# The second product as three float32r products, with all work in one list of steps

## The chip, the cores and the metric

The kernel runs on one core of a Trainium2 chip. Its time is the device time in microseconds (us) of one execution of the whole program. Before the change three executions took 589.52, 584.69 and 587.59 us, a median of 587.59 us.

The core has five engines, each with its own queue of instructions. TensorE multiplies matrices; the profile shows its matmuls as PE and the loading of their stationary operand as PEld. VectorE is DVE, ScalarE is ACT, GpSimd is POOL, and SyncE (SP) starts most of the DMA transfers. An engine works through its queue in order, and an instruction whose input is not there yet holds up everything behind it on that engine.

## The reference

Two parts follow each other. The first is a gated recurrence over 768 time steps, for 4 batches and 8 heads of 48 numbers; the second is a two-layer block on all 3072 tokens:

```python
f = 1.0 / (1.0 + np.exp(-f_logit))
for t in range(S):
    state = f[:, :, t, :, None] * state + np.einsum('bhd,bhe->bhde', k[:, :, t], v[:, :, t])
    y[:, :, t] = np.einsum('bhd,bhde->bhe', q[:, :, t], state)
...
h = x @ w_in                                                # (3072, 384) @ (384, 2048)
sp = np.maximum(h, 0.0) + np.log1p(np.exp(-np.abs(h)))
g = h * erf(sp)
return (g @ w_out).astype(np.float32)                       # (3072, 2048) @ (2048, 384)
```

`x` is `y` with the heads side by side, so a token has 384 numbers. The second product of the title is `g @ w_out`. Inputs and output are float32, except the two weight matrices, which come as 64-bit floats and are rounded to float32 on the chip.

## The kernel before

**Tiles and stages.** The 3072 tokens are 24 chunks of 128 (six to a batch); two chunks make a block of 256 tokens, so there are 12 blocks. For each chunk the recurrence is done as matrix products: running sums of the logarithms of the gates (`log_sums`, `tiled_sums`), their exponentials (`decays`), `q` and `k` scaled by them (`times_q`, `times_k`) and transposed, scores (`scores`, masked by `mask`), a state carried from half chunk to half chunk (`state_products`, `add_state`, copied by `copy_state`), and the rows of `x` (`x_rows`, `copy_x`). For each block, `half_group` makes the hidden values `h` in four groups of 512 hidden channels (six matmuls with 256 moving columns for half a group). A group then passes through a chain that changes between ACT and DVE: `copy_h` out of PSUM, an exponential and two tanh terms on ACT (`first`, `a_term`), two products on DVE (`times`, line 171), a tanh on ACT (line 677), and the last product on DVE (line 680), which leaves `g` in the place of `h`.

**The second product before.** Blocks 0 and 1 are multiplied plainly (`project_tile`, line 823): 32 float32 matmuls of 384 moving columns each. Blocks 2 to 11 use Strassen's rule in Winograd's form (`project`, line 870): seven products of half size in place of eight, 56 float32 matmuls of 192 columns for a block. The rule needs sums: `sum_w` makes four of `w_out` once, `sum_h` makes four of each group of `g` (DVE, line 761), and the seven products are put together by additions on DVE (line 878) and a copy on ACT (line 886).

**Weights.** `w_in` and `w_out` arrive as 16 pieces of 64-bit words. `round_piece` turns each into float32 by one pass on ACT and six on DVE (lines 346 to 369).

**What sets the order.** Until block 2's product the order of all work is the written list `EARLY`, a string of steps such as `h0_2` (block 0, half group 2) or `r5_3` (piece 5, rounding step 3). After it a loop over blocks takes the order from rules: the matmuls of `project(it - 2)` and then those of block `it + 1` are the slots, and at certain slots the loop calls `act_step` (one step of the ACT and DVE chain), `sum_step` (one sum) or `burst` (a whole chunk's recurrence work). PSUM, the memory that matmuls write to, is handed out by pools with rotating buffers: two pairs of banks for the products (`ps_moe`), one for the scores (`sc_all`), one for the rest.

**Start.** Until the first real matmuls are ready, `keep_busy` gives TensorE products of a constant tile with itself.

Of the kernel before, what the change touches and what calls it, by code (L numbers as in the profile page):

```python
# [44 lines left out]
FP32 = mybir.dt.float32  # L45
I32 = mybir.dt.int32
# [23 lines left out]
EXP_LN = 6  # L70

# [4 lines left out]
def kernel(  # L76
# [41 lines left out]
    w_out_sb = fixed("w_out_sb", [P, n_ft, d_model])  # L118
# [61 lines left out]
    xpool = main.enter_context(tc.tile_pool(name="xpool", bufs=2))  # L180
    epool = main.enter_context(tc.tile_pool(name="epool", bufs=2))
# [3 lines left out]
    singles = ExitStack()  # L185
    ps_at = [singles.enter_context(tc.tile_pool(name="ps_at", bufs=2, space=PSUM))]

    def bank(name):
        if len(ps_at) == 1:
            return ps_at[0].tile([P, 512], FP32, name=name, tag="at")  # L190
        return bank_pair(name)[:, 0, :]

    def bank_pair(name):
        return ps_at[1].tile([P, 2, 512], FP32, name=name, tag="at2")

    def open_pair():
        singles.close()
        ps_at.append(main.enter_context(tc.tile_pool(name="ps_at2", bufs=1, space=PSUM)))

    sc_all = ps_sc.tile([P, 2, 512], FP32, name="sc", tag="sc")  # L200

    NV, NQ, NG = 3, 3, 12
    ADJACENT = 5
    vts = [fixed(f"vt{i}", [P, d_model], pool=fix) for i in range(NV)]

# [9 lines left out]
    state = fixed("state", [P, HP, D], pool=fix)  # L215
    Hring = fixed("Hg", [P, NG * FG * TB], pool=fix)

    DH = d_model // 2
    NT = 4
    wT = fixed("wT", [P, n_g, NT * FG // 2 * DH], pool=fix)  # L220

    NS, NA = 3, 3
    S_WORDS = NS * NA * FG // 2 * P
    scratch = fixed("scratch", [P, S_WORDS + 5 * DH], pool=fix)
    sums_sb = scratch[:, 0:S_WORDS].rearrange("p (b n j t) -> p b n j t", b=NS, n=NA, j=FG // 2)
    rows_sb = scratch[:, S_WORDS:].rearrange("p (n c) -> p n c", n=5)

    def w_sums(gi):
        return wT[:, gi, :].rearrange("p (n j c) -> p n j c", n=NT, j=FG // 2)

    def h_group(blk, gi):

        if blk == 0:
            return wT[:, gi, 0 : FG * TB].rearrange("p (j t) -> p j t", j=FG)
        n = ((blk - 1) * n_g + gi) % NG
        return Hring[:, n * FG * TB : (n + 1) * FG * TB].rearrange("p (j t) -> p j t", j=FG)

    FIRST, SPLIT = 3, 4
# [25 lines left out]
    def load(g, what="qkv", queue=None):  # L264
        b, c = divmod(g, NCH)
        queue = queue or nc.sync
        for src, t, n in ((q, qns[g % NQ], "q"), (k, kns[g % NQ], "k")):
            if n in what:
                queue.dma_start(out=t[:].rearrange("t (h d) -> t h d", d=D), in_=heads(src, b, c))
        if "v" in what:  # L270
            queue.dma_start(
                out=vts[g % NV][:].rearrange("t (h d) -> t h d", d=D), in_=heads(v, b, c)
            )

    def copy_sv(g, r, c, engine):
        pairs = vts[g % NV][half(c)].rearrange("t (a r d) -> t a r d", r=2, d=D)
        copy_by(engine, svs[g % NSV][half(1 - r), r, c, :, PAD : PAD + D], pairs[:, :, r, :])
# [15 lines left out]
    rounded = set()  # L293

    HOMES = [("w", 0), ("w", 1), ("w", 2), ("w", 3), ("h", 4), ("h", 5), ("h", 6), ("h", 3)] + [
# [11 lines left out]
    def home_free(i):  # L309
        return all(x in rounded for x in range(i) if HOMES[x] == HOMES[i])  # L310
# [318 lines left out]
    def burst(g):  # L629
# [16 lines left out]
        if s:  # L646
            masks(g + 1)
# [697 lines left out]
```

## Time and profile before

| | |
|---|---|
| median of three executions | 587.59 us (584.69 to 589.52) |
| span of the profiled execution | 584.7 us, which is the time of the fastest of the three as far as it is shown; nothing measurable lies around the span |
| instructions | 14494 |
| PE (matmuls) busy | 572.8 us, 98% of the span |
| PEld (weight loads) busy | 503.7 us, 86% |
| DVE busy | 432.1 us, 74% |
| ACT busy | 383.9 us, 66% |
| POOL busy | 97.5 us, 17% |

In the rows of the trace that follow, a time stands in microseconds from the start of the span; `x24` is the number of instructions that a row gathers. A float32 matmul of the program stands in the trace as two matmul instructions with one weight load each, so the 56 matmuls of a Strassen block are 112 instructions. A group's row gives its busy time together, then the mean duration of one instruction in ns, then the idle time of the engine just ahead of them with what ended it. The chain of waits is the sequence of work that ended last, followed back from the end of the program.

### The profile page before, as it was taken

How to read it: one execution, taken by the hardware profiler on the slowest of the kernel's cores; microseconds unless marked ns; L12 is line 12 of the kernel's file. 1: busy time of each engine (PE TensorE's matmuls, PEld its weight loads, DVE VectorE, ACT ScalarE, POOL GpSimd, SP SyncE). 2: the span in 40 equal slices, each digit the busy share in tenths (PEclk: the TensorE clock that was granted, in tenths of full speed). 3: DMA queues.
4: the chain of work that ended last, by engine and by line, in shares of the span. 5: the costliest groups of instructions: out<-in, count | busy, mean ns of one | idle time of the engine just before them, and what ended most of it. 6: DMA issues, size and time to landing. Idle time of an engine off the chain costs nothing.

```text
span 584.7 us, 14494 instructions
## 1 busy us (share of the span) xinstructions
PE 572.8 (98%) x6039; PEld 503.7 (86%) x6039; DVE 432.1 (74%) x719; ACT 383.9 (66%) x482; POOL 97.5 (17%) x108
## 2 busy tenths in 40 slices
PE   8999999999999999999999999999999999999995
PEld 7778888887665889889889889889889989999995
DVE  5898988989988475876866867848688573938841
ACT  4867888888775658678677759666656556565300
POOL 2510103223120010322214112023043000000000
PEclk9989999999999999999999999999999999999999
DMA  9798746572355400143143143033010000000000
GB/s 213 167 259 202 192 87 151 145 150 68 58 102 89 81 3 1 30 83 55 29 82 55 30 83 56 29 54 56 28 29 16 28 1 2 29 0 2 28 27 31
DMA packets 153111, 41.39 MB, mean 71 GB/s; under 512 B 144848, under 2 KB 147920, under 8 KB 153040
## 3 DMA queue, kind: packets, MB, share of 16 engines
q1 hardware_dynamic: 150816, 39.81, 31.9%
q8 instruction: 49, 0.80, 0.6%
q10 hardware_dynamic: 2224, 0.59, 0.5%
q14 instruction: 22, 0.18, 0.1%
HBM read 35.59 MB, written 4.72 MB: 69 GB/s over the span
## 4 chain that ended last, share of the span: by engine, by line
PE 92%; DVE 3%; ACT 2%; DMA 1%; issue 1%; SPq 0%; DVEq 0%
PE hps L723 43%; PE ops L870 28%; PE ops L823 7%; PE y L616 4%; PE ps_t L484 2%; PE sc L550 2%; PE sc L539 2%; PE ps_d L435 1%; DMA w_out_sb<-in_moe_w_in_dram 1%; PE sc L558 1%; DVE scratch L761 1%; ACT x L166 1%; DVE qA L577 0%; PE sc L870 0%; DVE Hg L680 0%
## 5 line engine op out<-in xcount | busy, mean ns | idle before, releaser
L723 PE MATMUL hps<-xT,w_in_sb 128*128 128x256 f32 x1152 | 257.3, 382 | 0.0
L723 PEld LDWEIGHTS hps<-xT,w_in_sb 128*128 128x128 f32 x1152 | 218.2, 191 | 31.1 <-DVE w_in_sb L369 0.3
L171 DVE SCALAR_TENSOR_TENSOR e<-x,e 128x1024 f32<-128x1024 f32 x96 | 118.0, 1229 | 19.6 <-ACT x L166 19.4
L127 POOL COPY sv<-state 48x192 f32<-48x192 f32 x68 | 76.6, 1126 | 310.9 <-DVE state L518 239.4
L166 ACT ACTIVATE x<-Hg,serf_bias 128x1024 f32<-128x1024 f32 x88 | 97.6, 1139 | 0.4 <-DVE e L171 0.2
L163 ACT ACTIVATE e<-Hg 128x1024 f32<-128x1024 f32 x44 | 46.4, 1055 | 57.7 <-DVE Hg L680 57.5
L870 PE MATMUL ops<-wT,Hg 128*128 128x192 f32 x320 | 77.7, 326 | 0.0
L735 ACT COPY Hg<-hps 128x1024 f32<-128x1024 f32 x44 | 44.5, 1012 | 48.5 <-PE hps L723 48.3
L680 DVE TENSOR_TENSOR Hg<-Hg,e 128x1024 f32<-128x1024 f32 x44 | 53.7, 1220 | 22.1 <-ACT e L677 22.1
L870 PE MATMUL ops<-wT,scratch 128*128 128x192 f32 x288 | 67.8, 326 | 0.0
L870 PE MATMUL ops<-w_out_sb,Hg 128*128 128x192 f32 x320 | 65.8, 328 | 0.5 <-DVE scratch L878 0.5
L677 ACT ACTIVATE e<-e 128x1024 f32<-128x1024 f32 x48 | 50.3, 1048 | 9.1 <-DVE e L171 9.0
L870 PEld LDWEIGHTS ops<-wT,Hg 128*128 128x128 f32 x320 | 56.2, 190 | 0.1
L870 PEld LDWEIGHTS ops<-w_out_sb,Hg 128*128 128x128 f32 x320 | 53.9, 190 | 1.4 <-DVE scratch L878 0.8
L577 DVE TENSOR_TENSOR qA<-sc,tri 64x256 f32<-64x256 f32 x68 | 28.7, 422 | 34.6 <-PE sc L550 33.8
L870 PEld LDWEIGHTS ops<-wT,scratch 128*128 128x128 f32 x288 | 50.3, 190 | 0.3 <-ACT Hg L735 0.3
L878 DVE TENSOR_TENSOR scratch<-scratch,ops 128x384 f32<-128x384 f32 (+1 forms) x40 | 19.9, 498 | 35.2 <-ACT scratch L886 26.1
L870 PE MATMUL ops<-w_out_sb,scratch 128*128 128x192 f32 x132 | 32.3, 326 | 0.0
L494 ACT COPY qA<-ps_t 64x512 f32<-64x512 f32 x48 | 27.7, 577 | 4.3 <-PE ps_t L484 3.8
L616 PEld LDWEIGHTS y<-qA,sv 128*32 128x32 f32 x1408 | 20.7, 110 | 7.4 <-issue 6.7
L616 PE MATMUL y<-qA,sv 128*32 128x64 f32 x1408 | 24.3, 221 | 0.0
L870 PEld LDWEIGHTS ops<-w_out_sb,scratch 128*128 128x128 f32 x132 | 23.3, 190 | 0.0
(133 smaller groups left out, 642.7 us busy)
## 6 DMA issues: line engine op xcount, KB each, us to landing
qn<-in_q_dram SPq DMA_DIRECT2D x24, 192.0 KB, 3.5
kn<-in_k_dram SPq DMA_DIRECT2D x23, 192.0 KB, 3.8
vt<-in_v_dram SPq DMA_DIRECT2D x23, 192.0 KB, 3.3
out_dram<-scratch SPq DMA_DIRECT2D x11, 384.0 KB, 2.5
sv<-in_v_dram SPq DMA_DIRECT2D x84, 48.0 KB, 2.4
lt<-in_f_logit_dram SPq DMA_DIRECT2D x80, 48.0 KB, 2.6
w_out_sb<-in_moe_w_in_dram SPq DMA_DIRECT2D x4, 768.0 KB, 6.7
Hg<-in_moe_w_in_dram SPq DMA_DIRECT2D x4, 768.0 KB, 6.9
```

The lines of the kernel that those rows point to most:

```text
L127: (engine.copy if engine is nc.scalar else engine.tensor_copy)(out=out, in_=in_)
L163: nc.scalar.activation(out=dst[:], in_=h, func=AF.Exp)
L166: nc.scalar.activation(out=dst[:], in_=h, func=AF.Tanh, bias=serf_bias[:, i : i + 1], scale=SERF_KAB[i][0])
L171: nc.vector.scalar_tensor_tensor(out=e[:], in0=x[:], scalar=SERF_KAB[i][2], in1=e[:], op0=ALU.add, op1=ALU.mult)
L577: nc.vector.tensor_tensor(out=to, in0=sc[half(c), r], in1=tri1[half(c)].unsqueeze(1).broadcast_to((C, HP, C)), op=ALU.mult,)
L616: nc.tensor.matmul(y[M * i : M * (i + 1), kt, half(c)], lhsT=sv[:, r, c, a, o : o + M], rhs=qA[:, r, a, half(c)], start=(c == 0 and n == 0 ...
L677: nc.scalar.activation(out=e[0][:], in_=e[0][:], func=AF.Tanh, scale=SERF_C)
L680: nc.vector.tensor_tensor(out=h, in0=h, in1=e[0][:], op=ALU.mult)
L723: nc.tensor.matmul(hts[blk, gi][:, j, :], lhsT=w_in_sb[:, kt, ft * P : (ft + 1) * P], rhs=xTs[blk][:, kt, :], start=(kt == 0), stop=(kt == ...
L735: nc.scalar.copy(out=gr["h"], in_=hts.pop((blk, gi))[:])
L823: nc.tensor.matmul(ots[blk][:, tt, 0:d_model], lhsT=gr["h"][:, j, tt * P : (tt + 1) * P], rhs=w_out_sb[:, ft, :], start=(ft == 0), stop=(f ...
L870: nc.tensor.matmul(place[n], lhsT=x[:, j, :], rhs=y, start=(gi == 0 and j == 0 and n in first), stop=(gi == n_g - 1 and j == 1), skip_grou ...
```

## The change

**Three products.** A float32 number has 24 significant bits. The tile type `float32r` (`F32R`) keeps 12 of them when it is written. The new kernel writes `g` as two such parts, `ga` and `gb`, and `w_out` likewise, and takes the product from three matmuls on float32r tiles: `ga` times `form_c`, `gb` times `form_d`, and `gs` times `form_m`, where `gs` is `ga / 4096 + gb`, `form_c` is the high part of `w_out`, `form_d` 4096 times the difference, and `form_m` is `form_c - form_d`. The first two go into one pair of PSUM banks, the third into another, and the rows are the first sum times `1 - 1/4096` plus the second.

**What it costs in instructions.** Block 0 stays plain. Blocks 1 to 11 have 96 float32r matmuls of 384 moving columns each, against 64 (block 1) and 112 (blocks 2 to 11) matmul instructions before. Each group of `g` gets one more step on ACT (`part_a`, 1024 elements in each partition) and two on DVE (`part_b`, `part_s`). `w_out` gets four passes for each of its four groups (`form_c` on ACT; `form_u`, `form_d`, `form_m` on DVE, 1536 elements in each partition). Rows leave PSUM by `rows_first` on ACT and `rows_second` on DVE. All sums of Strassen's rule, the additions that put its products together and the two-part store of the last block are gone.

**One list.** `EARLY`, the loop and its rules (`act_step`, `sum_step`, `burst`, `late`) are replaced by `STEPS`, a list of all steps of the whole program. The new step names are `ka`, `kb`, `kt` (parts of `g`), `kc`, `ku`, `kD`, `kM` (parts of `w_out`), `o3_1_0_2` (block 3, group 1, tokens 0 to 127, third product), `ro` and `rp` (rows). A number behind `@` is the buffer: one of 13 SBUF slots of 1024 elements for `h`, the chain's tiles and the parts, or one of four pairs of PSUM banks. The state of the recurrence has two buffers in place of one, q and k are held for two chunks in place of three, and `keep_busy` has 18 products in place of 31.

```diff
+PART = 4096.0
+KAPPA = 4096.0 / 4095.5
...
-    ps_sc = main.enter_context(tc.tile_pool(name="ps_sc", bufs=1, space=PSUM))
-    ps_moe = main.enter_context(tc.tile_pool(name="ps_moe", bufs=2, space=PSUM))
...
+    def bank_pair(n):
+        return psum.tile([P, 2, 512], FP32, name=f"pair{n}", tag=f"pair{n}")
+
+    def slot(n, name, dtype=FP32):
+        return slots.tile([P, FG * TB], dtype, name=name, tag=f"slot{n}")
...
+    def form(t, gi):
+        n = f"{t}{gi // 2}"
+        if n not in formed:
+            formed[n] = parts.tile([P, 2, FG, d_model], F32R, name=f"form_{n}", tag=n)
+        return formed[n][:, gi % 2]
...
+    def form_c(gi):
+        nc.scalar.activation(out=flat_form("c", gi), in_=flat_plain(gi), func=AF.Copy, scale=KAPPA)
+
+    def form_u(gi):
+        nc.vector.tensor_tensor(
+            out=flat_plain(gi), in0=flat_form("c", gi).bitcast(FP32), in1=flat_plain(gi), op=ALU.subtract
+        )
+
+    def form_d(gi):
+        nc.vector.tensor_scalar(
+            out=flat_form("d", gi), in0=flat_plain(gi), scalar1=PART, scalar2=None, op0=ALU.mult
+        )
+
+    def form_m(gi):
+        nc.vector.tensor_tensor(
+            out=flat_form("m", gi), in0=flat_form("c", gi).bitcast(FP32),
+            in1=flat_form("d", gi).bitcast(FP32), op=ALU.subtract,
+        )
...
-    def sum_h(gr, sums=None):
-
-        while not gr["done"]:
-            act_step()
-        a11, a12, a21, a22 = blocks(gr["h"])
-        sums = sums or next(sum_places)
-        add(sums[0], a21, a22)
...
+    def part_a(blk, gi, n):
+        gps_[blk, gi] = [slot(n, "ga", F32R)]
+        nc.scalar.activation(out=gps_[blk, gi][0][:], in_=hs[blk, gi], func=AF.Copy, scale=KAPPA)
+
+    def part_b(blk, gi, n):
+        a = gps_[blk, gi][0]
+        gps_[blk, gi].append(slot(n, "gb", F32R))
+        nc.vector.tensor_tensor(
+            out=gps_[blk, gi][1][:], in0=hs[blk, gi], in1=a[:].bitcast(FP32), op=ALU.subtract
+        )
+
+    def part_s(blk, gi, n):
+        a, b = gps_[blk, gi]
+        gps_[blk, gi].append(slot(n, "gs", F32R))
+        nc.vector.scalar_tensor_tensor(
+            out=gps_[blk, gi][2][:], in0=a[:].bitcast(FP32), scalar=1.0 / PART, in1=b[:].bitcast(FP32),
+            op0=ALU.mult, op1=ALU.add,
+        )
...
+    def project(blk, gi, tt, *more):
...
+        acc = 1 if q == 2 else 0
...
+        for j in range(FG):
+            ft = gi * FG + j
+            if blk < N_PLAIN:
+                lhs, rhs = hs[blk, gi], plain(ft)[:, 0, :]
+            else:
+                lhs, rhs = gps_[blk, gi][q][:], form("cdm"[q], gi)[:, j, :]
+            nc.tensor.matmul(
+                ots[blk, acc][:, tt, 0:d_model],
+                lhsT=lhs.rearrange("p (j t) -> p j t", j=FG)[:, j, tt * P : (tt + 1) * P], rhs=rhs,
+                start=first and j == 0, stop=True, skip_group_check=True,
+            )
+
+    def rows_first(blk):
+        ps = ots[blk, 0][:, :, 0:d_model]
+        if blk < N_PLAIN:
+            nc.scalar.copy(out=rows_sb[:], in_=ps)
+        else:
+            nc.scalar.activation(out=rows_sb[:], in_=ps, func=AF.Copy, scale=1.0 - 1.0 / PART)
+
+    def rows_second(blk):
+        nc.vector.tensor_tensor(
+            out=rows_sb[:], in0=rows_sb[:], in1=ots[blk, 1][:, :, 0:d_model], op=ALU.add
+        )
...
-    def project(blk):
...
-        yield from products((0, 1), (1, 2, 6))
-        yield from products((0,), (5, 7, 3, 4))
-        to_sum.appendleft(sum_h(groups[blk, 3]))
...
+    STEPS = """
+        f0 v0 k0 q0 f1 in0 ms0 zb0@0 p0 q1 cl0 ex0 k1 ln0 v0_0_0g v1 z5 d0@1 v0_0_1g f2 v0_1_1g
...
+        ah3_3 f15 h4_3 ae4_0@9 am3_3 aw4_0@7 at4_0 ka3_3@4 sc11@2 au4_0 ds11 c4_1@12 o3_2_0_0
...
+        for token in STEPS:
+            name, numbers, engine, place = re.fullmatch("([a-zA-Z]+)([0-9_]+)([avg]?)(?:@([0-9]+))?", token).groups()
+            args = [int(n) for n in numbers.split("_")]
+            do[name](*args, *([ENGINE[engine]] if engine else []), *([int(place)] if place else []))
```

How the instructions move is seen at two places. The first is TensorE at a block's second product. Before, this is the place where the product of block 2 begins: the recurrence of a chunk (`ps_d`, `ps_t`), the hidden matmuls (`hps`), then the product (`ops`).

```order
L550 MATMUL sc<-qA,kT 64x64 x16
L435 MATMUL ps_d<-lt,tri_60 64x192 x4
L484 MATMUL ps_t<-ident,qd 128x64 x8
L484 MATMUL ps_t<-ident,kd_108 128x64 x8
L723 MATMUL hps<-xT,w_in_sb 128x256 x12
L870 MATMUL ops<-w_out_sb,Hg 128x192 x2
L870 MATMUL ops<-wT,scratch 128x192
```

In the new program the same queue stands as follows in the product of block 3. Every result has a name `pair` with a number, since all PSUM is handed out as pairs of banks; L703 is the second product, L627 the hidden matmuls, L553 and L541 scores and state products, L604 the rows of `x`.

```order
L703 MATMUL pair_2445<-form_m_1630,gs 128x384 x4
L627 MATMUL pair_2528<-xT,w_in_sb 128x256 x12
L553 MATMUL pair_2560<-qA,kT 64x64 x16
L541 MATMUL pair_2560<-vt_89,kd_98 64x48 x8
L703 MATMUL pair_2409<-form_c_1723,ga 128x384 x4
L703 MATMUL pair_2409<-form_d_1817,gb 128x384 x4
L703 MATMUL pair_2445<-form_m_1854,gs 128x384 x4
L604 MATMUL pair_2608<-qA,sv_91 32x64 x16
```

Before, the 112 instructions of the product stood together and a chunk's recurrence together between the hidden matmuls; now the product is cut into pieces of four matmuls with hidden and recurrence matmuls between them, and each piece reads a part of `g` that ACT or DVE makes shortly before.

The second place is DVE during block 2's product. Before, the chain (L171, L680) stands with the sums of `g` (L761) and the additions that put the products together (L878):

```order
L171 SCALAR_TENSOR_TENSOR e<-x,e 128x1024
L680 TENSOR_TENSOR Hg<-Hg,e 128x1024
L171 SCALAR_TENSOR_TENSOR e<-x,e 128x1024
L878 TENSOR_TENSOR scratch<-scratch,ops 128x384 x2
L878 TENSOR_TENSOR scratch<-scratch,ops 128x192
L761 TENSOR_TENSOR scratch<-Hg 128x256
L761 TENSOR_TENSOR scratch<-scratch,Hg 128x256
L171 SCALAR_TENSOR_TENSOR e<-x,e 128x1024
L761 TENSOR_TENSOR scratch<-Hg,scratch 128x256
L761 TENSOR_TENSOR Hg<-Hg 128x2x128
```

In the new program the chain is L176 and L659, `part_b` is L671, `part_s` L678 and `rows_second` L717:

```order
L671 TENSOR_TENSOR gb<-h,ga 128x1024
L659 TENSOR_TENSOR h<-h,e 128x1024
L176 SCALAR_TENSOR_TENSOR e<-x,e 128x1024 x2
L678 SCALAR_TENSOR_TENSOR gs<-ga,gb 128x1024
L671 TENSOR_TENSOR gb<-h,ga 128x1024
L717 TENSOR_TENSOR rows<-rows,pair_2095 128x768
L678 SCALAR_TENSOR_TENSOR gs<-ga,gb 128x1024
L449 TENSOR_TENSOR qd<-qn_93,dp_100 128x8x48
L456 TENSOR_TENSOR kd_98<-kn_95,kd_98 128x8x48
L659 TENSOR_TENSOR h<-h,e 128x1024
```

The four sums of 256 elements for a group have given way to two passes of 1024 elements, and one addition of 768 elements stands where five smaller ones stood.

More of the change, by code (lines that the diff above doesn't have):

```diff
@@ L45 @@
 FP32 = mybir.dt.float32
+F32R = mybir.dt.float32r
 I32 = mybir.dt.int32
@@ L710, with hidden_half @@
[L710 to L719 removed]
+        nc.scalar.copy(out=xTs[blk][:, :, j * P : (j + 1) * P], in_=yts[g][:])
+    hts, hs = {}, {}
+    def hidden_half(blk, p, n=None):
+        gi, i = divmod(p, 2)
+        if (blk, gi) not in hts:
+            hts[blk, gi] = bank_pair(n).rearrange("p b (j t) -> p (b j) t", t=TB)
+        for j in range(2 * i, 2 * i + 2):
```

911 lines of the change are left out of this document (345 added, 566 removed).

## The prediction

> **What bounds the kernel now.** I read the page's parts 1 and 4 first: busy time by engine, and the chain of waits by engine.
>
> ```profile
> PE 572.8 (98%) x6039; PEld 503.7 (86%) x6039; DVE 432.1 (74%) x719; ACT 383.9 (66%) x482; POOL 97.5 (17%) x108
> PE 92%; DVE 3%; ACT 2%; DMA 1%; issue 1%; SPq 0%; DVEq 0%
> ```
>
> TensorE is busy 98% of the span and is 92% of the chain, so fewer matmul cycles should shorten the time, as long as the others keep up. Whether they do is a matter of the stage, so I asked for windows. Columns: PE, PEld, DVE, ACT, POOL busy, granted clock, DMA share, GB/s.
>
> ```profile
> 0.00:60.00 60.00, 55.48 (x854) 46.98 (x855) 47.17 (x97) 41.25 (x76) 13.96 (x32) 0.97 0.93 209
> 60.00:120.00 60.00, 60.00 (x819) 51.36 (x819) 54.30 (x81) 52.65 (x71) 12.87 (x16) 1.00 0.58 137
> 120.00:180.00 60.00, 60.00 (x672) 42.16 (x670) 55.43 (x84) 49.37 (x65) 13.24 (x14) 1.00 0.49 100
> 60.00:80.00 20.00, 20.00 (x212) 17.57 (x212) 19.26 (x30) 16.57 (x23) 2.51 (x4) 1.00 0.69 168
> 259.68:304.96 45.28, 45.28 (x514) 41.36 (x513) 33.83 (x58) 31.84 (x38) 11.27 (x8) 1.00 0.29 54
> ```
>
> In a later block (last row) DVE has a quarter of its time left. Up to 180 us it has not: (54.30 + 55.43) / 120 = 91%, because the weights are rounded there. The chain in order of time shows what one block's 45.28 us consist of, and prices of single operations. Columns: start, us, what; the last two rows are from the early part.
>
> ```profile
> 259.68 18.40 PE ops L870 x112
> 278.08 5.18 PE hps L723 x24
> 283.26 1.03 PE y L616 x64
> ...
> 286.24 15.74 PE hps L723 x72
> ...
> 304.96 18.40 PE ops L870 x112
> ...
> 42.99 0.98 PE sc L558 x8
> ...
> 180.97 10.52 PE ops L823 x32
> ```
>
> Second product 18.40, hidden matmuls 5.18 + 15.74 = 20.92, a chunk's recurrence 286.24 − 283.26 = 2.98, twice: 45.28.
>
> **The float32r matmul's price.** No row shows one. Bounds: below, the eight instructions of `sum_totals` (L558), which load a full 128x128 tile and move only two columns, take 0.98 us, 0.1225 each, which is the pace of weight loads; above, a plain float32 matmul of the same 384 columns, 2 × 10.52 / 32 = 0.658. The nearest row is L870: an instruction there loads one 128x128 tile and takes 18.40 / 112 = 0.1643 for its 192 columns. Plain instructions with 384 columns take 10.52 / 32 = 0.329, twice that, so time goes by columns, and a float32 matmul of 192 is four passes of 192 in two instructions. One instruction of L870 is thus two passes of 192 columns behind one weight load; a float32r matmul is one pass of 384 columns behind one load. Both stream 384 columns, so I take 0.1643. The Trainium skill says on the page FP8 and Floating Point Precision (TensorE Precision Notes) that true FP32 takes four passes and that reduced precision reads a 4-byte FP32 and cuts it to FP22; that the second is one pass is nowhere in this trace.
>
> The weight of the sum is then simple. Blocks 2 to 11: 112 − 96 = 16 instructions less, 16 × 0.1643 = 2.63 us, ten times 26.3. Block 1: 64 × 0.329 = 21.0 becomes 96 × 0.1643 = 15.8, 5.3 less. TensorE has 31.6 us less to do. With everything else hidden the time would be 584.7 − 31.6 = 553 us. `keep_busy` fills waits for first data, so its 13 lost products count nothing.
>
> One rule speaks against it:
>
> ```profile
> L870 PEld LDWEIGHTS ops<-wT,Hg 128*128 128x128 f32 x320 | 56.2, 190 | 0.1
> ```
>
> A load lasts 0.190 us, so 112 of them end to end are 21.3 us, yet loads and matmuls of a block together take 18.40: the next load runs beside the matmul. The Trainium skill, on TensorE: Matmul & The Clock Gate (Part 3, The mechanism), holds that a weight load overlaps a running matmul only where the row group differs. Every instruction here uses all rows, so this trace contradicts it; it stays as a rival below.
>
> **What DVE and ACT get.** Group rows, from page part 5 and the grouping by line (after the bar: busy, mean ns):
>
> ```profile
> L171 DVE SCALAR_TENSOR_TENSOR e<-x,e 128x1024 f32<-128x1024 f32 x96 | 118.0, 1229 | 19.6 <-ACT x L166 19.4
> L163 ACT ACTIVATE e<-Hg 128x1024 f32<-128x1024 f32 x44 | 46.4, 1055 | 57.7 <-DVE Hg L680 57.5
> L680 DVE TENSOR_TENSOR Hg<-Hg,e 128x1024 f32<-128x1024 f32 x44 | 53.7, 1220 | 22.1 <-ACT e L677 22.1
> L577 DVE TENSOR_TENSOR qA<-sc,tri 64x256 f32<-64x256 f32 x68 | 28.7, 422 | 34.6 <-PE sc L550 33.8
> L878 DVE TENSOR_TENSOR scratch<-scratch,ops 128x384 f32<-128x384 f32 (+1 forms) x40 | 19.9, 498 | 35.2 <-ACT scratch L886 26.1
> L761 DVE TENSOR_TENSOR Hg<-Hg 128x256 f32<-128x256 f32 x40 | 16.7, 418 | 0.0
> L517 DVE TENSOR_TENSOR state<-sc,state 112x192 f32<-112x192 f32 x40 | 14.2, 355 | 5.2 <-POOL sv L127 2.0 <-PE sc L550 1.3 <-ACT qA L575 1.0
> L457 DVE TENSOR_TENSOR qd<-qn,dp 128x384 f32<-128x384 f32 x24 | 13.8, 574 | 0.0
> ```
>
> `part_b` costs like L680, `part_s` like L171, `part_a` like L163. A late block: DVE gains 4 × 2.45 = 9.8 and one addition of 768 (about 1.0), loses 16 sums of 0.42 and four additions of 0.50, 8.7: 33.8 + 2.1 = 35.9 us. ACT gains 4 × 1.055 and a row copy of 768 elements (three quarters of 1.055, 0.8) for one of 192 (0.3): 31.8 + 4.7 = 36.5. Both hide under TensorE's 45.28 − 2.63 = 42.65, with less room than they had.
>
> The early part is tighter. Before, block 2's product did not need `g` in parts and the sums of `w_out` were small; now 12 passes form `w_out`'s parts and blocks 1 to 3 need two passes a group. What a DVE instruction takes is seen in a full stretch (start, us):
>
> ```profile
> 63.74 0.55 DVE L346 TENSOR_SCALAR w_in_sb<-w_in_sb 128x768 f32<-128x768 f32 x1
> 64.20 0.95 DVE L369 TENSOR_TENSOR w_in_sb<-Hg,w_in_sb 128x768 f32<-128x768 f32 x1
> 65.08 0.55 DVE L350 TENSOR_SCALAR w_in_sb<-w_in_sb 128x768 uint32<-128x768 uint32 x1
> 65.54 0.56 DVE L346 TENSOR_SCALAR w_in_sb<-w_in_sb 128x768 f32<-128x768 f32 x1
> 66.02 0.95 DVE L355 SCALAR_TENSOR_TENSOR w_in_sb<-Hg,w_in_sb 128x768 uint32<-128x768 uint32 x1
> 67.00 0.56 DVE L359 TENSOR_SCALAR Hg<-w_in_sb 128x768 uint32<-128x768 uint32 x1
> 67.60 0.96 DVE L364 SCALAR_TENSOR_TENSOR Hg<-Hg 128x768 f32<-128x768 uint32 x1
> 68.48 0.55 DVE L350 TENSOR_SCALAR w_in_sb<-w_in_sb 128x768 uint32<-128x768 uint32 x1
> 68.95 1.22 DVE L171 SCALAR_TENSOR_TENSOR e<-x,e 128x1024 f32<-128x1024 f32 x1
> 70.08 0.95 DVE L369 TENSOR_TENSOR w_in_sb<-Hg,w_in_sb 128x768 f32<-128x768 f32 x1
> ```
>
> From start to start each takes 0.08 less than its duration (68.95 to 70.08 is 1.13), and about 0.04 more than its duration where the next reads its result (67.00 to 67.60). One piece's six passes come to about 4.25.
>
> I take one place of the new order, where group 3 of block 3 is first needed in its second part (`kb3_3` on DVE, `o3_3_0_1` on TensorE), and count what stands in DVE's queue up to it, start to start: 16 pieces 68.0; 73 passes of 1024 at 1.13, 82.5; eight passes of 1536 at 1.70 and four one-input ones at 0.94, 17.4; recurrence: 24 products at 0.49, 42 state steps at about 0.35, 20 masks at 0.34 and some 25 smaller ones, together 47. That is 215 us; with full durations (303 instructions, 0.08 each) it is 239. Both kinds occur in the rows, so 227.
>
> By 60 us DVE had done 47 us, held back by first data (DMA share 0.93), and I leave that. The remaining 180 at a share of 0.963 (row 60 to 80, the queue nearest to full) end at 60 + 187 = 247 us. From there TensorE still has 197 × 4 products at 0.1643 (129.5), 60 half groups at 20.92 / 8 = 2.62 (156.9), and 12 chunks at 2.98 (35.8): 322 us, ending at 569. The end, from the last matmuls:
>
> ```profile
> 577.93 0.35 DVE L878 TENSOR_TENSOR scratch<-scratch,ops 128x192 f32<-128x192 f32 x1 [0.56 <-PE ops L870]
> ```
>
> The span ends 6.8 us after this; `rows_second` is about 0.6 longer, which makes 577 us. If DVE is full without a gap and its price is the lower 215, the place comes at 228 and the end at 557; TensorE alone gives 553. Between 557 and 577 I stay nearer to the upper end, which rests on shares and prices that the rows show, and give back some for rounding that now stands earlier and can fill a part of the waits before 60 us: **569 us** for the profiled execution. The median stood 0.5% above it before (587.59 to 584.7), so **572 us**.
>
> So of 31.6 us some 16 arrive; the rest is lost while TensorE waits for DVE in the first 250 us.
>
> **Moves with one answer.** Two state buffers can take away the 2.0 us that L517 waited for POOL. q and k now have two buffers, so their loads cannot be issued more than two chunks ahead; a chunk comes every 22 us and a load lands in 3.5, so the loads stay covered. Ten states that ACT and DVE copied now go to POOL with the others:
>
> ```profile
> qn<-in_q_dram SPq DMA_DIRECT2D x24, 192.0 KB, 3.5
> L127 POOL COPY sv<-state 48x192 f32<-48x192 f32 x68 | 76.6, 1126 | 310.9 <-DVE state L518 239.4 <-DVE state L515 67.8 <-PE ps_d L616 1.6
> ```
>
> POOL has 310.9 us of idle time ahead of these copies. Two of 1.126 stand between a state and the rows that read it; on ACT two passes of 192 elements, under a fifth of L163's width, would by estimate take half of that. TensorE has hidden matmuls to do meanwhile; uncovered, ten states would cost some 12 us. `form_c` shares memory with block 0's `h`, so ACT waits at `kc0` for block 0's product of group 2; behind it stand `ka1_1` and `ax1_2`, needed for block 1. One step of the plain product is four matmuls of 0.658, 2.6 us, and TensorE has two more of them (`o0_3`) to cover it; uncovered it costs those 2.6 us.
>
> **The rivals.**
>
> *TensorE bounds throughout, 553 us* (549 to 557). For it: PE had no waits while DVE stood at 91%. Against it: the count above. Chance 0.20.
>
> *Finer pieces wait.* Before, 112 product instructions ran without a break and covered every handover. Now a piece of four lasts 4 × 0.1643 = 0.66 us, hidden pairs of banks must be copied out (about 1 us on ACT) before they are used again, and the product holds two of four pairs. One wait of 1 us a block adds 11 us to my 572: 581 to 588, near no change. For it: ACT's and DVE's 36 of 42.65 us. Chance 0.20.
>
> *Slower: DVE, not TensorE, sets the early part at a poor share.* The chain changes twice more between ACT and DVE for each group (`am` to `ka`, `ka` to `kb`), and both queues go in order. Price: (227 − 47) divided by the share. It is slower than 593 when the place comes later than 593 − 7 − 322 = 264 us, a share under 180 / 204 = 0.88; at 0.80 the end is 614. Against it: before had 0.91 with DVE not even the bound. Chance 0.10.
>
> *Weight loads in the open*: each of 1056 matmuls adds its 0.1225, so 553 + 129 = 682 us. It would follow from that overlap rule; chance 0.02. *Four passes after all*: 1056 × (0.658 − 0.1643) = 521 us more; chance 0.01. There the change would not do what it says.
>
> **How the numbers follow.** My case (558 to 580, DVE early, then TensorE) has 0.47. 552 to 590 leaves out the slow cases (0.12) and the lowest few (0.06). One per cent, about what a measurement here can tell, is 581.7 to 593.5: faster 0.47 + 0.20 and a fifth of the second rival, 0.71; same 0.16; slower 0.13.
>
> **What would show it.** A float32r matmul spaced 0.164 us, 15.8 us of product for a block. DVE over 95% busy between 60 and 240 us, and TensorE waiting there for `g` parts and rounded pieces, about 30 us in all; then TensorE at 100% with blocks of 42.7 us. Wrong if blocks after 300 us are longer than 44 us (second rival), or if TensorE has no waits before 240 us (first rival).

## The result: 5% slower

The changed kernel takes 616.7 us (median of four executions, 615.0 to 618.8) against 588.1 us for the kernel before beside it: a ratio of 1.050, 95% interval 1.045 to 1.055. The forecast was 572 us, with a range up to 590. The profiled execution has a span of 617.1 us.

First the page of the changed kernel: busy time of the engines, the granted clock in 40 slices, the chain by engine.

```profile
PE 584.0 (95%) x5885; PEld 501.3 (81%) x5885; DVE 481.7 (78%) x603; ACT 444.8 (72%) x524; POOL 86.5 (14%) x133
PEclk9988989999989999999999999999999999999998
PE 75%; DVE 13%; ACT 5%; issue 3%; POOL 1%; SPq 1%; DMA 0%; DVEq 0%; ACTq 0%; POOLq 0%
```

TensorE has 154 instructions fewer than before (5885 against 6039) and is busy 11 us longer. The windows, with the same columns as in the prediction, say where it waits:

```profile
0.00:60.00 60.00, 49.05 (x618) 39.88 (x619) 46.49 (x90) 34.30 (x54) 15.49 (x41) 0.91 0.88 213
60.00:120.00 60.00, 56.12 (x716) 44.11 (x714) 54.02 (x78) 40.67 (x61) 14.45 (x21) 0.97 0.57 145
120.00:180.00 60.00, 52.97 (x471) 40.13 (x471) 52.75 (x57) 46.42 (x55) 18.58 (x12) 0.94 0.23 44
180.00:240.00 60.00, 58.20 (x566) 52.19 (x565) 55.76 (x58) 52.63 (x60) 10.51 (x10) 1.00 0.20 37
300.00:420.00 120.00, 119.49 (x1191) 103.90 (x1189) 86.74 (x110) 87.04 (x100) 9.71 (x20) 1.00 0.27 51
```

In the first 240 us TensorE is idle for 24 us in all, and in the first 180 its clock is below 1; later it is full, with DVE and ACT far from it. The low clock stands in four stretches in which it was 0.50, 20.5 us together; the kernel before had one of 3.4 us (last row):

```profile
27.90:34.73 6.83, 6.83 (x22) 5.55 (x21) 5.57 (x10) 0.95 (x2) 0.00 (x0) 0.50 0.89 185
55.21:58.62 3.41, 3.41 (x31) 2.75 (x20) 3.27 (x5) 3.33 (x7) 0.47 (x1) 0.50 1.06 224
82.51:85.93 3.42, 3.42 (x8) 2.70 (x9) 3.35 (x6) 2.88 (x4) 0.00 (x0) 0.50 0.64 109
167.85:174.67 6.82, 5.10 (x75) 3.95 (x76) 2.38 (x3) 2.54 (x4) 2.30 (x3) 0.50 0.15 25
36.90:40.31 3.41, 3.41 (x12) 2.76 (x9) 2.94 (x8) 1.62 (x4) 0.74 (x1) 0.51 0.90 289
```

Even so, the late blocks are longer than before. `rows_first` stands in the list at a like place of each block; for blocks 5 and 10 it starts at

```profile
354.21 0.79 ACT L714 ACTIVATE rows<-pair 128x768 f32<-128x768 f32 x1
584.20 0.81 ACT L714 ACTIVATE rows<-pair 128x768 f32<-128x768 f32 x1
```

which is 229.99 / 5 = 46.0 us a block, against 45.28 before and 42.65 forecast, and TensorE waits only 1.0 us in these five blocks. So its instructions themselves are dearer. The chain of waits, which lies on TensorE there, prints the runs (start, us, what; L703 is the second product, L627 the hidden matmuls, L604, L553, L541, L480 and L427 the recurrence):

```profile
415.94 2.28 PE pair L703 x12
418.22 0.49 PE pair L427 x8
418.71 1.61 PE pair L703 x8
420.31 1.03 PE pair L604 x64
...
444.66 2.83 PE pair L703 x16
...
592.63 16.76 PE pair L703 x96
```

The same chain over two whole blocks, 354.1 to 447.3 us, by line:

```profile
by line: PE pair L627 44.2%; PE pair L703 39.8%; PE pair L604 5.5%; PE pair L480 2.8%; PE pair L541 2.6%; PE pair L427 2.6%; PE pair L553 2.3%; issue 0.3%
```

Half of those 93.1 us, by these shares, is a block: hidden matmuls 20.6, product 18.5, recurrence (five lines, 15.8%) 7.4, waits 0.1; together 46.6. This stretch holds 196 product instructions, four more than two blocks have, and four hidden ones less; counted for 96 of each, the product of a block takes 18.2 us and its hidden matmuls 21.0. The kernel before had 20.92 for the hidden matmuls, 18.40 for the product and 2 x 2.98 = 5.96 for the recurrence.

The last block's 96 product instructions run unbroken in 16.76 us, 0.1746 each, and the 16 behind hidden matmuls take 0.177 each. But a run that stands behind a piece of the recurrence costs 0.2 us on top: 12 x 0.1746 = 2.10, not 2.28; 8 x 0.1746 = 1.40, not 1.61.

The whole of TensorE's time can be split that way: each row of its timeline costs the time to the start of the next row, less the wait noted there. Where the kind of matmul changes, this books a part of the time to the neighbouring kind, so the split between kinds is good to a few us; the totals do not depend on it.

| us | before | after |
|---|---|---|
| hidden matmuls | 254.9 | 255.7 |
| second product | 225.9 | 223.4 |
| recurrence | 82.0 | 98.0 |
| `keep_busy` | 10.0 | 7.3 |
| TensorE's instructions | 572.9 | 584.4 |
| waits | 3.3 | 23.4 |

The product became 2.5 us cheaper where the forecast had 31.6. The recurrence, of which no instruction was added, became 16 us dearer. Counted from the end of one row to the end of the next, the product falls by about 5, the recurrence rises by 14, and the hidden matmuls rise by 5. And there are 20 us of new waits, 22 of the 23.4 us before 260 us.

Against the kernel before, then, most was lost early. The two spans differ by 32.4 us (the medians by 28.6, since this execution of the changed kernel is the slowest of its four and that of the kernel before the fastest). 20 us of it are waits. TensorE was busy for 18.8 us at half its clock, against 3.4 us before, which by estimate (half of the difference) makes its instructions some 8 us dearer. About 4 us are left for everything else on TensorE: the dearer recurrence, less what the product and `keep_busy` save.

### The profile page after: what moved, and what is told of

It is laid out like the page before. It is cut to its first block, busy times and chain, and to the rows that moved or that the text cites. A ratio compares the mean times of both kernels' runs of the same rounds, so it can differ in the third digit from the quotient of the medians.

```text
span 617.1 us, 14290 instructions
## 1 busy us (share of the span) xinstructions
PE 584.0 (95%) x5885; PEld 501.3 (81%) x5885; DVE 481.7 (78%) x603; ACT 444.8 (72%) x524; POOL 86.5 (14%) x133
## 4 chain that ended last, share of the span: by engine, by line
PE 75%; DVE 13%; ACT 5%; issue 3%; POOL 1%; SPq 1%; DMA 0%; DVEq 0%; ACTq 0%; POOLq 0%
PE pair L627 33%; PE pair L703 28%; PE pair L604 4%; PE pair L541 2%; DVE e L176 2%; PE pair L480 2%; PE pair L553 2%; DVE qA L578 1%; PE pair L427 1%; PE pair L561 1%; DVE early_m L341 1%; DVE state L522 1%; ACT qA L576 1%; ACT x L171 1%; PE pair L471 1%
## 5 line engine op out<-in xcount | busy, mean ns | idle before, releaser
L627 PE MATMUL pair<-xT,w_in_sb 128*128 128x256 f32 x1152 | 266.7, 387 | 7.4 <-ACT kd L436 2.5
L627 PEld LDWEIGHTS pair<-xT,w_in_sb 128*128 128x128 f32 x1152 | 220.1, 193 | 41.9 <-ACT kd L436 4.0
L176 DVE SCALAR_TENSOR_TENSOR e<-x,e 128x1024 f32<-128x1024 f32 x96 | 117.3, 1224 | 29.2 <-ACT e L168 19.5
L171 ACT ACTIVATE x<-h,serf_bias 128x1024 f32<-128x1024 f32 x88 | 100.3, 1145 | 5.1 <-PE pair L703 1.6
L703 PE MATMUL pair<-form_c,ga 128*128 128x384 f32 x352 | 81.1, 352 | 1.3 <-DVE rows L717 1.3
L703 PE MATMUL pair<-form_m,gs 128*128 128x384 f32 x352 | 80.0, 350 | 0.0
L703 PE MATMUL pair<-form_d,gb 128*128 128x384 f32 x352 | 77.2, 341 | 0.0
L659 DVE TENSOR_TENSOR h<-h,e 128x1024 f32<-128x1024 f32 x44 | 54.0, 1228 | 19.9 <-ACT e L655 19.7
L671 DVE TENSOR_TENSOR gb<-h,ga 128x1024 fp32r<-128x1024 f32 x44 | 54.5, 1239 | 14.2 <-ACT ga L666 10.4
L703 PEld LDWEIGHTS pair<-form_m,gs 128*128 128x128 f32 x352 | 62.4, 190 | 3.5 <-issue 2.1
L703 PEld LDWEIGHTS pair<-form_c,ga 128*128 128x128 f32 x352 | 60.5, 188 | 5.2 <-issue 2.3
L703 PEld LDWEIGHTS pair<-form_d,gb 128*128 128x128 f32 x352 | 61.9, 188 | 1.4 <-DVE gs L678 0.3
L678 DVE SCALAR_TENSOR_TENSOR gs<-ga,gb 128x1024 fp32r<-128x1024 f32 x44 | 54.1, 1230 | 3.5 <-PE pair L703 1.9
L604 PEld LDWEIGHTS pair<-qA,sv 128*32 128x32 f32 x1536 | 26.1, 112 | 18.8 <-issue 6.4
L604 PE MATMUL pair<-qA,sv 128*32 128x64 f32 x1536 | 32.1, 225 | 9.6 <-POOL qA L585 5.1
```

The source lines that it names most:

```text
L171: nc.scalar.activation(out=dst[:], in_=h, func=AF.Tanh, bias=serf_bias[:, i : i + 1], scale=SERF_KAB[i][0])
L176: nc.vector.scalar_tensor_tensor(out=e[:], in0=x[:], scalar=SERF_KAB[i][2], in1=e[:], op0=ALU.add, op1=ALU.mult)
L604: nc.tensor.matmul(y[M * i : M * (i + 1), kt, half(c)], lhsT=sv[:, r, c, a, o : o + M], rhs=qA[:, r, a, half(c)], start=(first and n == 0) ...
L627: nc.tensor.matmul(hts[blk, gi][:, j, :], lhsT=w_in_sb[:, kt, ft * P : (ft + 1) * P], rhs=xTs[blk][:, kt, :], start=(kt == 0), stop=(kt == ...
L659: nc.vector.tensor_tensor(out=h, in0=h, in1=es.pop((blk, gi))[:], op=ALU.mult)
L671: nc.vector.tensor_tensor(out=gps_[blk, gi][1][:], in0=hs[blk, gi], in1=a[:].bitcast(FP32), op=ALU.subtract)
```

## The experiments

All times are medians; the kernel before took 586 to 588 us beside them.

**The two kinds of matmul alone (`pace`).** A kernel of nothing but runs of matmuls, and of turns between two kinds:

```python
# float32r, 384 columns, four in a row into one bank
for i in range(64):
    mm(banks[i // 4 % 6][:, 0:384], lhsT=gr[:, i % 8, :], rhs=wr[:, wide(i, 384)], **first(i))
...
# four float32r of 384 and 32 small ones in turn
for n in range(8):
    for i in range(4):
        mm(banks[n % 3][:, 0:384], lhsT=gr[:, i % 8, :], rhs=wr[:, wide(i, 384)], **first(i))
    small(32)
```

> Only the two kinds of matmul, no kernel around them (all other work is left out). Theory A, the price on TensorE was too low: a float32r matmul of 384 columns takes 0.175 us from start to start in an unbroken run (0.164 was forecast), and a run of full-size matmuls that follows small ones (64x64 stationary, 48 columns) starts 0.2 us late whatever its kind, so four float32r and 32 small ones in turn cost about 4 x 0.175 + 0.2 + 0.51 to 0.61 = 1.4 to 1.5 us a turn, and sixteen in place of four add 12 x 0.175 = 2.1 us; float32r and float32 of 256 columns in turn cost nothing extra, 4 x 0.175 + 6 x 0.432 = 3.29 us a turn. Theory B, the pace is as forecast and pieces of the kernel wait for others: 0.164 us here, and turns cost the sum of their parts. Where the extra 0.010 us comes from: a fixed part of each instruction gives about 0.121 us at 256 and 0.228 at 512 columns; a lower rate for every column gives 0.116 and 0.233; if it is the sum into one bank four times in a row, a new bank each time gives 0.164; if it is the changing stationary tile, one tile gives 0.164.

The chain of `pace` (start, us, line). L130, L133, L136 are float32r with 384 columns: into one bank, into a new bank each, with one stationary tile. L139 has 512 columns, L142 256. L145 and L148 are float32 with 192 and 256, two instructions a matmul. L154 and L156 are float32r and float32 in turn; L160 and L165 runs of 4 and 16 float32r between small ones (L112), L170 a run of six float32 matmuls of 256 columns between them. The granted clock is 1.00 over all these rows.

```profile
29.88 11.10 PE bank L130 x64
40.98 11.09 PE bank L133 x64
52.07 11.09 PE bank L136 x64
63.17 14.55 PE bank L139 x64
77.72 7.67 PE bank L142 x64
85.39 10.40 PE bank L145 x64
95.79 13.81 PE bank L148 x64
109.61 15.06 PE bank L112 x512
...
128.17 0.70 PE bank L154 x4
128.87 2.59 PE bank L156 x12
...
153.88 0.90 PE bank L160 x4
154.78 2.00 PE bank L112 x64
...
174.18 2.98 PE bank L165 x16
...
194.10 2.79 PE bank L170 x12
```

A float32r matmul of 384 columns takes 11.09 / 64 = 0.1733 us, whatever the bank and the stationary tile. A float32 instruction that also streams 384 columns (two passes of 192) takes 10.40 / 64 = 0.1625. From 384 to 512 streamed columns both grow alike, by 0.054 and 0.053 us, so the difference of 0.011 us is a fixed part of each float32r instruction. At 256 columns 7.67 / 64 = 0.1198 is found, the pace of weight loads that the prediction had as its lower bound (0.1225), so that point decides nothing. The Trainium skill, on TensorE: Matmul & The Clock Gate (Part 2, Back-to-back issue gap), gives N / 2.4 + 2.5 ns as the gap of matmuls taken by themselves, from which 162.5 ns at 384 and 215.8 ns at 512 columns follow. It adds that a stream with its weight loads goes faster at 512 columns, about 131 ns. The rows here are such streams and do not go faster: the float32 rows agree with the first formula to the digit (0.1625, and 13.81 / 64 = 0.2158), and float32r's 0.1733 and 0.2273 are 11 ns above it.

Float32r and float32 in turn cost the sum of their parts (0.70 and 2.59). Behind small matmuls four float32r take 0.90 in place of 0.70, and sixteen 2.98 in place of 2.77: 0.2 us once a run. It is not a matter of float32r: six float32 matmuls take 2.79 behind small ones and 2.59 behind float32r. The small ones lose 0.12 behind big ones (2.00, against 64 x 15.06 / 512 = 1.88). A turn costs 2.90 and not the 1.4 to 1.5 that I had written: my small float32 matmuls are two instructions of 0.029 each. The timeline at such a change, with the weight loads (PEld):

```profile
153.49 0.26 PEld L112 LDWEIGHTS bank<-w,g 64*64 64x64 f32 x6
153.81 0.65 PEld L160 LDWEIGHTS bank<-wr,gr 128*128 128x128 f32 x4
```

The first full load (0.188 us) starts only when the small loads and matmuls are about done, so nothing covers it. That 0.2 us is this load is argued from these rows; no run takes the load away.

**More changes of kind (`more_switches`).** Two small matmuls ahead of 128 product pieces:

```diff
+        if blk >= 4 and q < 2:
+            for n in range(2):
+                nc.tensor.matmul(
+                    ots[blk, acc][0:C, n, d_model : d_model + D], lhsT=ident[0:C, 0:C],
+                    rhs=tri[0:C, 0:D], start=True, stop=True, skip_group_check=True,
+                )
```

> The changed kernel with two small matmuls more (64x64 stationary, 48 columns, into columns of PSUM that nobody reads) ahead of each piece of the first and second product of blocks 4 to 11: 128 times, 94 of them behind a big matmul. Nothing else changes. Theory A: the small ones themselves cost 2 x 0.029 us, and each place behind a big matmul another 0.32 us (0.12 for the change to small ones, 0.20 for the change back): 7.5 + 30 = 37.6 us more, 654 us. Theory B (time goes to handovers between engines, changes of kind cost nothing): 7.5 us more at most, 617 to 624 us.

675.3 us, 58.6 more than the changed kernel. The chain (L709 is the product, L699 the new small ones):

```profile
381.94 0.20 PE pair L699 x4
382.13 0.90 PE pair L709 x4
383.04 0.36 PE pair L699 x4
383.39 0.90 PE pair L709 x4
```

A place behind big matmuls costs 0.36 + 0.20 = 0.56 us for two small matmuls, one behind other small ones 0.20. 94 x 0.56 + 34 x 0.20 = 59.4 us. Theory B had at most 7.5. The direction is A's; its price was too low, again because each small matmul is two instructions, and because a run as short as this takes longer to start (0.16 us more than behind small ones).

**Fewer changes (`grouped`), no DVE parts (`no_parts`), both.** The same steps in another order, so that small matmuls stand together (at chunks 13 and 14):

```diff
-ds13@1 sc13 ... y13_0@0 ... y13_1 ... d14@0 ... e14 ...
+ds13@0 sc13 d14@3 e14 ... y13_0@3 ... y13_1 ...
```

> The changed kernel with another order of the same steps: log_sums of a chunk moved up to the scores of the chunk before, transposes up to the rows of the chunk before, so that small matmuls stand together. From chunk 8 on TensorE changes 63 times from big matmuls to small ones and back, in place of 86; nothing is left out. Theory A (each run of small matmuls between big ones costs 0.2 us at its end and about 0.1 at its start): 23 x 0.3 = 7 us less than the changed kernel, about 610 us. Theory B (the pieces' handovers between engines cost the time): the product pieces that covered a handover now stand elsewhere, so no gain, or some us more than 617.

614.0 us, 2.7 less than the changed kernel; single executions of either lie 3 to 4 us apart. TensorE's instructions fell by 6.5 us to 577.9, as A had it; waits rose by 3.1. In the five late blocks the exchange is plain: 20 runs of the product start behind small matmuls in place of 36, TensorE's instructions take 3.5 us less and its waits 4.3 us more, and a block still takes 46.2 us. After 350 us TensorE's waits in `grouped` are

```profile
PE pair L553 <- DVE state L522: 3.1, 3, 2.0
PE pair L553 <- DVE kT L132: 0.9, 3, 0.5
```

where the changed kernel waited 1.1 us altogether. The product pieces between two steps of a chunk had covered the way over ACT and DVE. Without them there is a wait.

```diff
-        nc.vector.tensor_tensor(
-            out=gps_[blk, gi][1][:], in0=hs[blk, gi], in1=a[:].bitcast(FP32), op=ALU.subtract
-        )
+        nc.gpsimd.memset(gps_[blk, gi][1][:].bitcast(FP32), 0.25)
```

(`part_s` likewise.)

> The changed kernel with part_b and part_s left out: DVE does not compute gb and gs, POOL fills their tiles with a constant, the matmuls stay. DVE has 44 x 2.45 = 108 us less to do. Theory A (TensorE is the bound after 260 us and its instructions are dearer than forecast): blocks after 300 us stay at 46 us, and only the first 260 us gain, at most the 13 us that TensorE waits there after the first 60 us; 602 to 612 us. Theory B (handovers to DVE and ACT make the late blocks long): blocks after 300 us fall towards 43 us and the time to 590 us or less.

609.4 us. 108 us less on DVE are worth 7.3 us, and all of it is gained early: blocks 5 to 10 still take 45.9 us each. So DVE is not what makes the late blocks long.

> Both edits at once: the order of grouped and the missing part_b and part_s of no_parts. grouped took 6.5 us from TensorE's instructions and gave 3 to 4 back as waits for DVE's copies and states (lines 132 and 522) after 350 us. If these waits come from DVE's queue being full of parts, both gains stand here: 609.4 less 6.5, about 603 us, and the waits after 350 us go. If they come from the length of the handovers themselves, the waits stay and the time is 606 to 607 us.

608.6 us, 0.8 less than `no_parts`, where the order alone had gained 2.7. Most of the waits did not go with DVE's work: 4.9 us of the 6.1 that `grouped` has after 260 us stay. So they come in the main from the length of the handovers, not from a full queue.

**States back to ACT and DVE (`states_back`).** In the list, five of the ten tokens become `sp0a` and the like, five `sp8v` and the like:

```diff
-        st1 sp0g ln1 v3
+        st1 sp0a ln1 v3
```

> The changed kernel with the ten copies of the state that the kernel before gave to ACT (0, 5, 6, 7, 17) and DVE (8, 9, 10, 20, 22) given back to them; nothing else changes and nothing is left out. If these copies on POOL, ahead of its selects, cost the early part (rows L604 wait 5.1 us for POOL's select and 1.5 us for its copies), the time falls by 3 to 7 us, to 610 to 614 us. If POOL only hands on what DVE delays, DVE has 5 x 0.7 us more in its full stretch and the time is 617 us or a little more.

617.3 us: no difference. That part of the change costs nothing.

**The product alone, in the order of the kernel before.** The kernel before with its product changed and Strassen's sums of `g` left on DVE, without readers; the parts of `g` and of `w_out` are left out, so this is the cost of the matmuls alone:

```diff
+        for acc in range(2):
+            for gi in range(n_g):
...
+                for part in range(2 - acc):
+                    for tt in range(CPB):
+                        for j in range(FG):
+                            nc.tensor.matmul(
+                                ops[acc][:, tt, 0:d_model],
+                                lhsT=g_r[gi][:, tt * P : (tt + 1) * P],
+                                rhs=w_r[:, j % 3, :],
...
+        nc.scalar.copy(out=g_r[gi][:], in_=gr["h"][:, 0, :])
```

> The kernel before with only the product of blocks 2 to 11 changed: 96 float32r matmuls of 384 columns in one unbroken run, in its own order. They read one float32r piece of g per group and three of w_out, so the parts of g and w_out are left out; the sums of Strassen's rule stay on DVE without a reader, and rows leave by one ACT and one DVE pass. Theory A (0.175 us each, and what was lost besides was lost by cutting the product into pieces): a block's product takes 96 x 0.1746 + 0.2 = 17.0 us in place of 18.4, ten blocks 14 us less, 573 to 575 us. The forecast's price (0.1643): 16.0 us a block, 24 us less, 564 us. If float32r costs as much as Strassen's rule however it is placed: 588 us.

608.3 us, since the product waited 24.7 us for my copy in ACT's queue. With the copy on DVE:

> As before_f32r, which was slower than the kernel before because its product waited 24.7 us for a copy that I had put into ACT's queue (g_r, line 788). Here the same copy stands on DVE, directly behind the last product of the chain, where Strassen's sums stood; the rest is the same, and the parts are left out as there. Theory A (0.175 us for a float32r matmul, no loss in an unbroken run): a block's product takes 17.0 us in place of 18.4, and if the wait is gone, ten blocks give 14 us, 572 to 575 us. If the product still waits for its input, the block's TensorE time is 1.4 us less all the same and the rest shows as waits. If a float32r product costs as much as Strassen's rule even unbroken: 587 us without waits.

578.5 us, 1.4% faster than the kernel before (ratio 0.986, interval 0.981 to 0.991).

```profile
348.50 16.87 PE ops L857 x96
```

TensorE's instructions sum to 559.0 us, 13.9 less than before, as A had it; 4.5 of that went into more waits (7.8 us against 3.3). A float32r product in an unbroken run does gain. What it lacks here is its parts. With their work put in:

```diff
+        nc.scalar.activation(out=pa, in_=h, func=AF.Copy, scale=4096.0 / 4095.5)
+        yield
+        nc.vector.tensor_tensor(out=pb, in0=h, in1=pa, op=ALU.subtract)
+        yield
+        nc.vector.scalar_tensor_tensor(
+            out=pa, in0=pa, scalar=1.0 / 4096.0, in1=pb, op0=ALU.mult, op1=ALU.add
+        )
+        nc.vector.tensor_copy(out=g_r[gi][:], in_=pa[:, 0:TB])
```

> before_f32r_dve with the work of the parts put in: in place of Strassen's four sums, each group of blocks 2 to 11 has one ACT pass and two DVE passes of 1024 elements (part_a, part_b, part_s), which all groups write to the same two places, and DVE copies a piece of the last one for the product to read. What is left out is that the product reads all of the parts, and the parts of w_out. So this is the product and its work in the unbroken order of the kernel before, only with no room to keep the parts. TensorE's instructions should stay at 559 us. If the loss lies in the cut and interleaved order of the list, the waits stay near the 7.8 us of before_f32r_dve and the time at 578 to 583 us. If the chain through ACT (an ACT pass, two DVE passes ahead of each group's product) needs the cover that the list gives it, the product waits as in before_f32r (24.7 us) or longer, and the time is 600 us or more.

632.8 us. Part of this was my doing (one place for all groups), so:

> As before_parts, which waited 35.2 us for g_r; its ACT pass (line 790) stood idle 52.4 us for the last DVE pass of the group before, because all groups shared one place, and ACT's queue stood still behind it. Here the groups take two places in turn and part_b writes in place, so ACT runs ahead. If that sharing was the cause, most of the 46.3 us of waits go and the time is 580 to 595 us. If an ACT pass and two DVE passes ahead of each group's product are too long a chain for the order of the kernel before in any case, 20 us of waits or more stay, and the time is above 600 us.

619.7 us, with 34.9 us of waits. ACT's pass now stands idle for the shared place for 6.5 us in place of 52.4, so the sharing was a part of it, but most of the product's waits remain:

```profile
PE ops L857 <- DVE g_r L797: 31.0, 11, 5.9
326.57 11.09 PE L857 MATMUL ops<-w_r,g_r 128*128 128x384 f32 x48 [3.76 <-DVE g_r L797]
325.18:326.57 1.39, 0.00 (x1) 0.00 (x1) 1.36 (x3) 1.36 (x2) 0.00 (x0) 0.50 0.95 187
326.57:331.57 5.00, 5.00 (x16) 5.00 (x17) 2.56 (x3) 4.00 (x5) 0.00 (x0) 0.50 0.01 4
332.00:337.66 5.66, 5.66 (x34) 5.66 (x33) 2.81 (x3) 4.34 (x6) 0.00 (x0) 1.00 0.00 0
```

The order of the kernel before has no cover for an ACT pass and two DVE passes ahead of each group's product. And a wait costs more than its length, which the other rows show: TensorE waits 3.76 us from 322.81 on, the granted clock is 0.50 from 325.18 to 332.00, and TensorE starts 16 instructions in 5 us, 0.31 us each.

No version with all of the computation was found that beats the kernel before. The unbroken product with its full parts was not built, so what it would take stays open.

## Why the prediction was wrong, point by point

**The step that failed: "Both stream 384 columns, so I take 0.1643."** Two things are wrong in that term. The pace is 0.1746 and not 0.1643: the columns were right, the 0.011 us that a float32r instruction takes besides was not seen in any row of before. And the price came from a run of 112 instructions, into which the one loss of 0.2 us at its start had been averaged (112 x 0.1625 = 18.2, not 18.40); that loss is paid for each run, and the list starts a run behind small matmuls 15 times in the two blocks after 354 us. A block's product was forecast at 15.8 us. It took 18.2 there: 96 x 0.1746 = 16.8, and 7.5 starts of 0.2 make 1.5. Strassen's 112 instructions took 18.40, so the saving was eaten before it arrived.

**"12 chunks at 2.98 (35.8)"** failed for the same reason. These pieces stood in one run a chunk; now each stands between big matmuls. They take 7.4 us a block in place of 5.96, and over the whole kernel, with the slow clock early on, 16 us more.

**The forecast's sum.** It had 247 us for the place where group 3 of block 3 is ready, and 322 us of TensorE after it, an end at 577 with the tail, from which I gave back 8.

```profile
257.12 1.22 DVE L671 TENSOR_TENSOR gb<-h,ga 128x1024 fp32r<-128x1024 f32 x1
```

This is `kb3_3`: 10 us late. The last product instruction ends at 609.4, 352 us after it: 30 us more, of which the product makes 20 (197 x 4 x 18.2 / 96 = 149 against 129.5), the recurrence 8 to 9 (12 x 3.7 = 44 against 35.8) and waits 1.7. With the 8 us given back for nothing that is 48, the whole of the miss.

**The early part.** DVE's work up to that place was counted at 227 us; its windows sum to about 225. Its share after 60 us was 0.91, not 0.963. DVE above 95% was thus wrong, and so was DVE as the only cause: `no_parts` took 29 us from it before block 4 and gained 7; the wait for POOL's `qA` in the first row below is 4.6 us shorter there. TensorE's waits before 260 us are many small ones; the largest, with all from before 260 us (us in total, times, longest):

```profile
PE pair L604 <- POOL qA L585: 5.1, 3, 3.2
PE pair L627 <- ACT kd L436: 2.5, 2, 1.5
PE pair L553 <- ACT kT L132: 1.9, 1, 1.9
PE pair L627 <- ACT xT L614: 1.8, 1, 1.8
```

The forecast of about 30 us of waits was near (22), their cause only in part: 17 us of them stand in `no_parts` too, and no run shows what makes them. What the waits cost through the clock (0.91, 0.97 and 0.94 in the first three windows, by the estimate above 8 us more than before) was not in the sum.

**What was right.** The passes cost what their neighbours did:

```profile
L671 DVE TENSOR_TENSOR gb<-h,ga 128x1024 fp32r<-128x1024 f32 x44 | 54.5, 1239 | 14.2 <-ACT ga L666 10.4
L666 ACT ACTIVATE ga<-h 128x1024 fp32r<-128x1024 f32 x44 | 46.3, 1053 | 20.0 <-DVE h L659 19.6
L678 DVE SCALAR_TENSOR_TENSOR gs<-ga,gb 128x1024 fp32r<-128x1024 f32 x44 | 54.1, 1230 | 3.5 <-PE pair L703 1.9
```

1.24 and 1.23 us for L680's 1.22 and L171's 1.23, 1.05 for L163's 1.055. They are hidden late, as forecast, and the ten states on POOL cost nothing.

**The rivals.** "Finer pieces wait" named the right thing, the pieces, and its sign came (blocks longer than 44 us), but not its mechanism: there are no waits late, the pieces cost TensorE time in themselves. "DVE at a poor share" had its bound at 264 us, and the place came at 257; with the forecast's 322 us behind it and the tail of 8 that alone gives an end at 587, about the time of the kernel before. "Weight loads in the open" at each matmul is refuted (0.1746 with loads of 0.188); once a run, behind small matmuls, a load in the open is what the rows of `pace` suggest. "Four passes after all" is refuted by 0.1733 us for a whole matmul. "TensorE bounds throughout" fell with the waits.

**Where the gain went.** The product's 14 us exist (`before_f32r_dve`). The parts put a longer chain ahead of each group's product; in the old order this chain stops TensorE (34.9 us of waits, a slow clock behind them, 619.7 us). After 260 us the list covers such chains by laying product pieces between the small steps, and pays for the cuts with TensorE time; before that it does not cover all its handovers and loses 22 us in waits (616.7 us). `grouped` moved along that exchange and gained 2.7 us. That no order of this work does much better is not shown.

## What to carry to other kernels

Price a matmul from a run as long as the one that it will stand in, and price the starts of runs separately: here a run of full tiles behind small ones cost 0.2 us, and the small ones between big ones another 0.1 to 0.16. A product that saves 14% of its instructions, each a little dearer, lost that when it had to start behind small matmuls seven or eight times a block. And when work is moved ahead of an operand (parts, sums, casts), count the engines that it passes through as well as its microseconds: three passes on two engines cost more as a chain than as work.

## What the runs showed of the hardware that I had not expected

A float32r instruction takes 0.011 us more than a float32 instruction that streams as many columns (0.1733 against 0.1625 at 384, 0.2273 against 0.2158 at 512). Behind 3.76 us of waiting the granted clock was 0.50 for 5.4 us, and 48 product instructions took 11.09 us where another execution without the wait shows 8.62 (`before_f32r_dve`, at 267.62 us). The Trainium skill, on TensorE: Matmul & The Clock Gate (Part 1, What's actually happening), says that the clock halves after an idle window of about 3.4 us and returns after one of work. The trace agrees in kind, not in the lengths: here it had halved 2.4 us after the last matmul and came back 5.4 us after the next. Changing between float32r and float32 matmuls of full tiles cost nothing (0.70 and 2.59 us in turn, as in unbroken runs).
